# The order of the two halves of P beside the FFN: POOL's half first, VectorE's second

## The chip, the cores and the metric

The kernel runs on one core of a Trainium2 chip. The metric is the device time of one execution in microseconds; of the kernel before there are three: 980.2 (median), 979.35 and 982.82. One further execution was profiled; it took 981.36 us, and its span, from the first to the last instruction in the trace, is 979.6 us. In the profile PE is TensorE's matmuls and PEld its weight loads, DVE is VectorE, ACT is ScalarE, POOL is GpSimd and SP the engine that issues most DMAs. L468 is line 468 of the kernel's file.

## What is computed

Attention whose mask comes from a hash, and on its output an FFN with a gate:

```python
# q, k, v: (4, 8, 768, 64) f32; proj: (64, 6); w_in: (512, 2048); w_out: (2048, 512)
q_bits = einsum('bhsd,dk->bhsk', q, proj) > 0        # 6 bits: 64 buckets; k alike
mask   = q_bucket[:, :, :, None] == k_bucket[:, :, None, :]
scores = where(mask, (q @ k.T) / 8, -1e9)
attn   = exp(scores - max) ; attn /= attn.sum() + 1e-9
x      = (attn @ v) as (3072, 512)                    # tokens x (heads * 64)
h      = x @ w_in
out    = (h * clip(h + 3, 0, 6) / 6) @ w_out
```

All is float32. The kernel multiplies float32 numbers as pairs: a high part, which is the number rounded to the type that TensorE reads (`fp32r` in the profile), and a low part, the rest. A product is the sum of high and low terms, so before each product an engine makes the high part with a copy and another the low part with a subtraction.

## The kernel before

Attention is cut into blocks g of 128 queries of one head: 6 blocks a head, 32 heads, 192 blocks. P is the 128 x 768 tile of exponentials of one block. The FFN is cut into chunks of 256 tokens, each of 16 steps over d_ff, 128 columns a step (`gemm1` L642, the gate L664 and L665, its two parts L670 and L671, `gemm2` L680 to L685). The FFN of the first batch runs early; that of the later ones runs beside the attention of the blocks behind block 102 (`GT`), one FFN step to each attention step k, in the function `beside_ffn`. The order of all instructions on PE, DVE, ACT and POOL is that of the program, written out by hand; only DMAs are issued with dependences of their own. An engine takes its instructions in this order and waits at each until its operands are there.

In a step k of `beside_ffn` with k of at least 102 this is issued, in this order:

- if k is odd, `values_whole(u)`: the product of V with P of the two blocks 2u and 2u + 1 (2u + 3 is k or, at the ends, less). On PE it is 12 matmuls into one accumulator (L501): the high parts of P, keys 0 to 383 (half c = 0), then keys 384 to 767 (c = 1), then the low parts in the same order;
- `lowest(k + 2)` on VectorE (L385): scores from the accumulator to SBUF, with their minimum;
- the two parts of the gate of the FFN step before: copy on ACT (L670), subtraction on VectorE (L671);
- `exponential(k + 2)` on ACT (L397), and on VectorE the transpose of its result in blocks of 32 x 32 (`flip`, L418), whose result goes to DRAM and comes back with whole rows and columns exchanged (tiles `px` and `spare` by turns, `move`);
- `split_p(k - 1, c)` for c = 0 and then c = 1: from the tile that came back it makes the high part `ph` with a copy on ACT (L464), and the low part `pl` of half 0 on VectorE (L468) and of half 1 on POOL (L466). POOL's subtraction is issued at once, VectorE's is kept in the list `lows` and issued behind both copies (`split_lows`);
- `gemm1` of the FFN step on PE; the output of attention, if there is one (L528 to L531); in every sixth step the hash of the next head (`hash_qk` on PE, and after the gate `bits`, L341 on VectorE);
- `gemm2` of the FFN step before on PE, and the gate of this one: L664 on ACT and L665 on VectorE;
- `scores(k + 3)` on PE (L376, L378), DMAs, and every second or third step a subtraction for the next head's q and k on POOL (L318).

Each pair of blocks u has four tiles, `ph` and `pl` for each half; each of the names has two buffers, so that the tiles of a pair take over those of the pair before, once its products have read them.

Of the kernel before, what the change touches and what calls it, by code (L numbers as in the profile page):

```python
# [43 lines left out]
def lsh_attention_moe(  # L44
# [10 lines left out]
    nc = tc.nc  # L55
# [3 lines left out]
    KT = S // P  # L59
    HW = S // 2  # L60
    QT = HW // P
# [31 lines left out]
    def bank(shape, name: str, tag: str | None = None):  # L93

        nonlocal turn
        if tag is None:
            tag = ("pt", "pu")[turn % 2]
            turn += 1
        return ps.tile(shape, F32, name=name, tag=tag, bufs=2)
# [280 lines left out]
    def lowest(g: int):  # L380

        s = scs.pop(g)
        m = sp.tile([P, 1], F32, name=f"m{g}", tag="m", bufs=4)
        pr_ = sp.tile([P, 2, HW], F32, name=f"p{g}", tag="p", bufs=2)
        nc.vector.tensor_scalar(  # L385
            out=pr_[:], in0=s[:, :, :HW], scalar1=CAP, scalar2=None,
            op0=ALU.min, op1=ALU.min, accum_out=m[:],
        )
        probs[g] = pr_, m

    def exponential(g: int):
        i, t = divmod(g, KT)
        b, h = divmod(i, H)
        if b not in sms:
            sms[b] = sp.tile([P, KT, H], F32, name=f"sms{b}", tag="sms", bufs=2)
        pr_, m = probs[g]
        nc.scalar.activation(  # L397
            pr_[:], pr_[:], AF.Exp, bias=m[:], scale=-1.0, accum_out=sms[b][:, t, h : h + 1]
        )
# [4 lines left out]
    def transp(g: int, c: int):  # L404
        pt = pts[g, c] = bank([P, QT, P], f"pt{g}_{c}")
        for x in range(QT):
            nc.tensor.transpose(pt[:, x], probs[g][0][:, c, x * P : (x + 1) * P], ident[:])  # L407
        if c:
            del probs[g]
# [30 lines left out]
    def split_p(g: int, c: int, third: bool):  # L440

        nonlocal halves
        u, w = divmod(g, 2)
        if w == 0:
            extra = third and halves % 3 == 1
            halves += 1
            if extra and lent:
                both = [x[:, :S] for x in lent]
            else:
                both = [  # L450
                    sp.tile([P, NCC * TC if extra else S], F32R, name=f"{x}{u}_{c}", tag=f"x{x[1]}" if extra else x, bufs=1 if extra else 2)[:, :S]
                    for x in ("ph", "pl")
                ]
            parts[u, c] = [x.rearrange("p (x w q) -> p x w q", x=QT, w=2) for x in both]
        hi, lo = (x[:, :, w] for x in parts[u, c])
        engine = nc.vector
        if g < GT:
            pt = pts.pop((g, c))[:]
        else:
            pt = moved[g].rearrange("p (i x a) -> p x i a", i=4, x=KT)[:, c * QT : (c + 1) * QT]  # L460
            hi, lo = (x.rearrange("p x (i a) -> p x i a", i=4) for x in (hi, lo))
            if c:
                engine = nc.gpsimd
        nc.scalar.copy(hi, pt)  # L464
        if engine is nc.gpsimd:
            engine.tensor_sub(lo, pt, hi.bitcast(F32))  # L466
        else:
            lows.append(lambda: engine.tensor_sub(lo, pt, hi.bitcast(F32)))  # L468
# [3 lines left out]
    def split_lows():  # L472
        for f in lows:
            f()
        lows.clear()
# [18 lines left out]
    def values_whole(u: int):  # L494
        vv = vvs[2 * u // KT]
        acc = accs[u] = bank([P, 2 * P], f"acc{u}")
        both = [parts.pop((u, c)) for c in range(2)]
        for part in range(2):
            for kt in range(KT):
                c, x = divmod(kt, QT)  # L500
                nc.tensor.matmul(  # L501
                    acc[:], lhsT=vv[:, kt], rhs=both[c][part][:, x],
                    start=(part == 0 and kt == 0), stop=(part == 1 and kt == KT - 1),
                )

    adds = []

    def add():
        for _, to, of in adds:
            nc.gpsimd.dma_start(out=to, in_=of, accum_op=ALU.add)  # L510
        adds.clear()

    def output(un: int):
        nonlocal vdone
        i, u = divmod(un, KT // 2)
        b, h = divmod(i, H)
        o = (h % 2) * D
        acc = accs.pop(un)

        if u != 1:  # L520
            outs[i] = sp.tile([P, 4 * P if u == 0 else 2 * P], F32, name=f"y{i}_{u}", tag=f"y{u}", bufs=1)
        y = outs[i][:, 2 * P :] if u == 1 else outs[i][:, : 2 * P]

        r = slice(o, o + D)
        r2 = slice(D - o, 2 * D - o)
        last_head = h == H - 1 and (b > 0 or u == 2)
        if last_head:
            nc.scalar.copy(y[r], acc[r2])  # L528
            nc.vector.tensor_add(y[r], acc[r], y[r])
        else:  # L530
            nc.scalar.copy(y, acc[:])  # L531
        if u or last_head:
            c = slice(2 * u * P, 2 * (u + 1) * P) if last_head and b else slice(0, 4 * P) if u == 1 else slice(4 * P, S)
            to = xs[b][h * D : (h + 1) * D, c]

            with tc.issue_after(copied.ins):
                dma(out=to, in_=y[r] if last_head else outs[i][r])
            if not last_head:
                adds.append((i, to, outs[i][r2]))
        vdone = 2 * un + 2  # L540
# [38 lines left out]
    def multiply():  # L579
        for f in muls:  # L580
            f()
        muls.clear()
# [468 lines left out]
    def value_whole():  # L1051
        nonlocal vnext
        values_whole(vnext // 2)
        vnext += 2

    def value_half():
        nonlocal vnext
        u, c = divmod(vnext, 2)
        vnext += 1
        values(u, c)  # L1060
        return c == 1
# [14 lines left out]
    with tc.manual_schedule(engines={ET.PE, ET.DVE, ET.Activation, ET.Pool}):  # L1076
# [9 lines left out]
        def go(part: str):  # L1086
            if stage == part:
                next(fill, None)
# [3 lines left out]
        def beside_ffn(k: int):  # L1092

            nonlocal paced, stage, held
            held = False
            if k < GT:
                for c in range(2):
                    transp(k, c)  # L1100
                exponential(k + 1)
            for _ in range(2):
                u = vnext // 2
                if u < NS // 2 and (2 * u < GT or k % 2 and k >= 2 * u + 3):
                    if vnext % 2 == 0 and k >= GT:
                        value_whole()
                        through.append(u)
                        break
                    if value_half():
                        through.append(vnext // 2 - 1)  # L1110
                if k < GT:
                    break
            if k == GT:
                opening.pop()()
            if k + 2 < NS and k >= GT:
                lowest(k + 2)
            go("A")
            if k < GT:
                for c in range(2):
                    split_p(k, c, False)  # L1120
                split_lows()
                while through:
                    output(through.pop(0))
                flip(k + 1)
            if k + 2 < NS:
                if k < GT:
                    lowest(k + 2)
                exponential(k + 2)
            paced = True
            multiply()  # L1130
            if k + 2 < NS:
                flip(k + 2)
            if GT <= k - LT < NS:
                for c in range(2):
                    split_p(k - LT, c, False)
            split_lows()
            go("B")
            if k == NS + LT:
                homes.clear()
            while through and (through[0] < vnext // 2 - 1 or k % 2 == 0 or k < GT):  # L1140
                output(through.pop(0))
            hashed = k + LA < NS and (k + LA) % KT == 4 and (k + LA) // KT + 1 < NJ
            if hashed:
                hash_qk((k + LA) // KT + 1)
            go("C")
            if hashed:
                bits((k + LA) // KT + 1)
            if k + LA < NS:
                lead(k + LA)
            if moves:  # L1150
                moves.pop(0)()
            if GT <= k + 1 < NS:
                move(k + 1)

            place_in_chunk = (k - GT) % NFC
            if subs and (k % 2 and (k < GT or place_in_chunk != NFC - 1) or k > GT and place_in_chunk == 0):
                subs.pop(0)()
            go("D")
            if k % KT in (1, 3):
                add()  # L1160

        for k in range(NS + LT + 2):
# [3 lines left out]
            end = GB if k < GB else NS  # L1166
# [65 lines left out]
            if k + 1 == GB:  # L1232
                first = first_ffn(lambda part: ahead(GB, part))
# [57 lines left out]
```

## Time and profile before

| | |
|---|---|
| median of 3 executions | 980.2 us |
| the profiled execution | 981.36 us |
| its span | 979.6 us |
| stretch in which attention and FFN run side by side | 405 to 806 us |
| granted TensorE clock, mean of the span | 0.998 |
| L466 (POOL's low part) in the stretch: 86, mean of one | 1388 ns (from `spare`), 1378 ns (from `px`) |
| L468 (VectorE's low part) in the stretch: 86, mean of one | 519 ns, 517 ns |
| L464 (copies on ACT) in the stretch: 172, mean of one | 504 ns |

A row of the timeline has the start in us from the start of the span, the length in us, the engine, the line, the operation, what it writes and reads, the shapes, and how many alike are merged; the brackets hold the idle time of the engine ahead of it and what ended that. A row of the groups has busy us and mean ns behind the first bar, and idle us and its releasers behind the second. A row of the waits has who waited for whom, the total in us, how often, and the longest. The chain of waits is followed back from the last instruction, each step to what released it.

### The profile page before, as it was taken

Reading aid. Unit: us, or ns where it says so; the run is one execution under the profiler, and the core shown is the slowest. Engines: PE = TensorE matmul, PEld = TensorE weight load, DVE = VectorE, ACT = ScalarE, POOL = GpSimd, SP = SyncE. Lnnn points to the kernel's source line nnn. Section 1 sums busy time; section 2 is a strip of 40 time slices with the busy share of each in tenths; the row PEclk is TensorE's granted clock in tenths of the full one; section 3 lists DMA queues with packets and bytes.
Section 4 is the critical chain, followed back from the end, with each engine's and each line's share of the span. In section 5 each row is a group of like instructions: output and inputs, shape, how many; then the busy total and the mean of one; then the engine's idle time right before and its main releaser. Section 6 shows DMA issues by size and latency. Waiting matters only on the chain.

```text
span 979.6 us, 19386 instructions
## 1 busy us (share of the span) xinstructions
PE 953.1 (97%) x6306; PEld 874.4 (89%) x6306; DVE 715.7 (73%) x1462; ACT 626.7 (64%) x1421; POOL 479.2 (49%) x498
## 2 busy tenths in 40 slices
PE   8999999999999998899999999999999999999997
PEld 7999888999989998799889888998999899899896
DVE  7999988888569998777777777877777874343422
ACT  6898875656478897567766666766766664333332
POOL 6777744656537775355555545546556542000000
PEclk9999999999999999999999999999999999999999
DMA  4566579100035554687797787797797772101000
GB/s 118 138 165 174 132 229 376 46 2 1 6 121 130 117 114 118 184 246 235 217 274 231 230 244 234 225 272 231 233 267 228 220 222 78 43 1 44 1 22 22
DMA packets 113116, 151.65 MB, mean 155 GB/s; under 512 B 13764, under 2 KB 82116, under 8 KB 113016
## 3 DMA queue, kind: packets, MB, share of 16 engines
q1 hardware_dynamic: 108456, 144.79, 48.8%
q0 software_dynamic: 4560, 5.64, 4.6%
q8 instruction: 50, 0.82, 0.4%
q14 instruction: 50, 0.41, 0.1%
HBM read 77.34 MB, written 53.61 MB: 134 GB/s over the span
## 4 chain that ended last, share of the span: by engine, by line
PE 77%; DVE 9%; issue 4%; POOL 3%; DMA 3%; ACT 2%; SPq 1%; DVEq 0%; ACTq 0%; POOLq 0%
PE h L642 25%; PE po L685 6%; PE po L680 6%; PE po L681 6%; PE acc L489 6%; PE acc L501 5%; PE s L376 5%; PE pt L407 5%; PE s L378 5%; DVE p L385 3%; DVE pl L468 2%; POOL pl L466 2%; DVE qq L341 1%; DMA px<-fd 1%; SPq L78 1%
## 5 line engine op out<-in xcount | busy, mean ns | idle before, releaser
L397 ACT ACTIVATE p<-p,m 128x768 f32<-128x768 f32 x192 | 180.2, 938 | 97.0 <-DVE p L385 91.3
L385 DVE TENSOR_SCALAR_CACHE_REDUCE p<-s 128x768 f32<-128x768 f32 x192 | 183.0, 953 | 45.4 <-PE s L378 30.8
L665 DVE SCALAR_TENSOR_TENSOR h<-g,h 128x256 f32<-128x256 f32 x192 | 81.9, 427 | 95.2 <-ACT g L664 93.5
L664 ACT ACTIVATE g<-h,three 128x256 f32<-128x256 f32 x192 | 90.8, 473 | 91.4 <-PE h L642 89.7
L642 PE MATMUL h<-xh,w 128*128 128x256 f32 x1024 | 146.8, 283 | 1.6 <-ACT xh L631 1.6
L642 PEld LDWEIGHTS h<-xh,w 128*128 128x128 f32 x1024 | 135.5, 189 | 5.1 <-ACT xh L631 1.8
L418 DVE STREAM_TRANSPOSE p<-p 128x768 f32<-128x768 f32 x90 | 88.0, 978 | 60.3 <-ACT p L397 60.3
L466 POOL TENSOR_TENSOR pl<-spare,ph 128x384 fp32r<-128x384 f32 x45 | 62.1, 1381 | 119.0 <-ACT ph L464 82.8
L376 PE MATMUL s<-kk,qq 76*128 76x384 f32 x384 | 101.4, 345 | 4.8 <-DVE qq L341 3.0
L468 DVE TENSOR_TENSOR pl<-pt,ph 128x384 fp32r<-128x384 f32 x196 | 100.0, 550 | 3.6 <-ACT ph L464 3.0
L670 ACT CAST gb<-h 128x256 fp32r<-128x256 f32 x141 | 52.4, 372 | 76.1 <-DVE h L665 43.1
L378 PE MATMUL s<-kk,qq 128*128 128x384 f32 x384 | 100.6, 343 | 0.0
L681 PE MATMUL po<-w,gb 128*128 128x512 f32 x250 | 98.4, 394 | 0.0
L680 PE MATMUL po<-w,gb 128*128 128x512 f32 x250 | 98.4, 394 | 0.0
L466 POOL TENSOR_TENSOR pl<-px,ph 128x384 fp32r<-128x384 f32 x45 | 61.3, 1362 | 75.2 <-ACT ph L464 66.0
L464 ACT CAST ph<-pt 128x384 fp32r<-128x384 f32 x196 | 85.9, 472 | 15.1 <-PE pt L407 13.1
L216 POOL TENSOR_TENSOR w<-wr,w 128x128 fp32r<-128x128 f32 x128 | 71.8, 591 | 45.3 <-ACT w L210 42.4
L407 PE MATMUL pt<-ident,p 128*128 128x128 f32 x612 | 86.0, 274 | 3.6 <-DVE pl L468 2.7
L407 PEld LDWEIGHTS pt<-ident,p 128*128 128x128 f32 x612 | 71.7, 141 | 11.2 <-PE pt L407 2.5
L376 PEld LDWEIGHTS s<-kk,qq 76*128 76x128 f32 x384 | 65.7, 190 | 17.9 <-DVE qq L341 8.0
L642 PE MATMUL h<-xl,w 128*128 128x256 f32 x512 | 81.5, 281 | 0.0
L685 PE MATMUL po<-w,gb 128*128 128x512 f32 x250 | 78.7, 395 | 0.0
(153 smaller groups left out, 2130.9 us busy)
## 6 DMA issues: line engine op xcount, KB each, us to landing
fd<-p SPq DMA_DIRECT2D x90, 384.0 KB, 3.0
spare<-fd SPq DMA_DIRECT2D x180, 96.0 KB, 2.6
px<-fd SPq DMA_DIRECT2D x180, 96.0 KB, 3.2
kk<-qq SPq DMA_DIRECT2D x62, 192.0 KB, 3.3
wr<-in_w_in SPq DMA_DIRECT2D x16, 512.0 KB
wr<-in_w_out SPq DMA_DIRECT2D x16, 512.0 KB, 7.5
raw<-in_qkT SPq DMA_DIRECT2D x19, 384.0 KB, 3.8
vr<-in_v SPq DMA_DIRECT2D x32, 192.0 KB, 3.4
```

What stands on the lines that cost most here:

```text
L376: nc.tensor.matmul(s[:, c, :HW], lhsT=q1[:KM, us], rhs=half(k1[:KM], c), start=True, stop=False)
L378: nc.tensor.matmul(s[:, c, :HW], lhsT=q2[:, us], rhs=half(k2, c), start=False, stop=True)
L385: nc.vector.tensor_scalar(out=pr_[:], in0=s[:, :, :HW], scalar1=CAP, scalar2=None, op0=ALU.min, op1=ALU.min, accum_out=m[:],)
L397: nc.scalar.activation(pr_[:], pr_[:], AF.Exp, bias=m[:], scale=-1.0, accum_out=sms[b][:, t, h : h + 1])
L407: nc.tensor.transpose(pt[:, x], probs[g][0][:, c, x * P : (x + 1) * P], ident[:])
L466: engine.tensor_sub(lo, pt, hi.bitcast(F32))
L468: lows.append(lambda: engine.tensor_sub(lo, pt, hi.bitcast(F32)))
L642: nc.tensor.matmul(hp, lhsT=wi[:, wp, wc], rhs=x[cc][xp], start=(k == 0 and cc == 0), stop=(k == 2 and cc == NCC - 1),)
L664: nc.scalar.activation(r[:], hp, AF.Relu, bias=three[:], scale=1.0)
L680: nc.tensor.matmul(po[u], lhsT=gh[:, us], rhs=wo[:, 0], start=(fc == 0), stop=False)
L681: nc.tensor.matmul(po[u], lhsT=gh[:, us], rhs=wo[:, 1], start=False, stop=False)
L685: nc.tensor.matmul(po[u], lhsT=gl[:, us], rhs=wo[:, 0], start=False, stop=(fc == NFC - 1))
```

## The change

In every step of `beside_ffn` from block 102 on the halves are split in the order c = 1, c = 0, and `values_whole` multiplies in that order too, the high parts of half 1 and half 0 and then the low parts of half 1 and half 0. The `start` and `stop` flags of the accumulation move to the new first and last matmul. The rest of the program is as it was: the subtraction of half 0 is still issued behind both copies, and in the earlier part of the kernel the halves keep their order.

```diff
@@ values_whole
         both = [parts.pop((u, c)) for c in range(2)]
+        first, end = (0, 1, 0), (1, 0, QT - 1)
         for part in range(2):
-            for kt in range(KT):
-                c, x = divmod(kt, QT)
-                nc.tensor.matmul(
-                    acc[:], lhsT=vv[:, kt], rhs=both[c][part][:, x],
-                    start=(part == 0 and kt == 0), stop=(part == 1 and kt == KT - 1),
-                )
+            for c in (1, 0):
+                for x in range(QT):
+                    nc.tensor.matmul(
+                        acc[:], lhsT=vv[:, c * QT + x], rhs=both[c][part][:, x],
+                        start=(part, c, x) == first, stop=(part, c, x) == end,
+                    )
@@ beside_ffn
             if GT <= k - LT < NS:
-                for c in range(2):
+                for c in (1, 0):
                     split_p(k - LT, c, False)
             split_lows()
```

## The prediction

> **What bounds the kernel now.** I read the page first, for which engine is full, then the stretch from 405 to 806 us, the only one in which the changed lines run side by side with the FFN.
>
> ```profile
> PE 953.1 (97%) x6306; PEld 874.4 (89%) x6306; DVE 715.7 (73%) x1462; ACT 626.7 (64%) x1421; POOL 479.2 (49%) x498
> ```
> ```profile
> 405.00:806.00 401.00, 394.80 (x2534) 360.63 (x2532) 304.31 (x588) 266.27 (x619) 217.39 (x189) 1.00 0.81 238
> ```
>
> In that stretch (the second row, busy us of PE, PEld, DVE, ACT and POOL in turn) PE is busy 394.8 of 401 us, so TensorE bounds by its own work; VectorE is busy 304.3. But a share says nothing of order, so next the timeline of two neighbouring steps (start, length, engine, line, in brackets the idle time before and its releaser).
>
> ```profile
> 722.06 0.91 ACT L464 CAST ph<-px 128x384 fp32r<-128x384 f32 x2
> 722.19 0.98 DVE L418 STREAM_TRANSPOSE p<-p 128x768 f32<-128x768 f32 x1 [0.64 <-ACT p L397]
> 723.06 1.42 POOL L466 TENSOR_TENSOR pl<-px,ph 128x384 fp32r<-128x384 f32 x1 [2.29 <-ACT ph L464]
> 723.09 0.52 DVE L468 TENSOR_TENSOR pl<-px,ph 128x384 fp32r<-128x384 f32 x1
> 723.64 0.43 DVE L665 SCALAR_TENSOR_TENSOR h<-g,h 128x256 f32<-128x256 f32 x1
> 723.98 0.95 DVE L385 TENSOR_SCALAR_CACHE_REDUCE p<-s 128x768 f32<-128x768 f32 x1
> 726.04 0.98 DVE L418 STREAM_TRANSPOSE p<-p 128x768 f32<-128x768 f32 x1 [0.76 <-ACT p L397]
> 726.94 0.52 DVE L468 TENSOR_TENSOR pl<-spare,ph 128x384 fp32r<-128x384 f32 x1
> ...
> 728.69 0.96 DVE L385 TENSOR_SCALAR_CACHE_REDUCE p<-s 128x768 f32<-128x768 f32 x1 [0.90 <-PE s L378]
> ```
>
> Follow VectorE: minimum (L385), then the exponential on ACT that it must wait for, transpose (L418), low part (L468), gate (L665), next minimum. It is a ring (the transpose's releaser is the exponential, L397): from L468 at 723.09 to L468 at 726.94 are 3.85 us, with no idle time but the wait for the exponential, which sits inside the ring. The only slack of the pair is the 0.90 before L385 at 728.69, where TensorE's scores are late. So a second ring runs almost as slowly as TensorE, and L468, which the change delays, is a link of it.
>
> Every sixth step also hashes the next head, and there VectorE is not slack at all:
>
> ```profile
> 577.51 0.52 DVE L468 TENSOR_TENSOR pl<-spare,ph 128x384 fp32r<-128x384 f32 x1
> 577.95 0.42 DVE L665 SCALAR_TENSOR_TENSOR h<-g,h 128x256 f32<-128x256 f32 x1
> 578.40 1.08 DVE L341 TENSOR_SCALAR qq<-z,thr,val 44x768 fp32r<-44x768 f32 x1
> 579.54 0.62 PE L376 MATMUL s<-kk,qq 76*128 76x384 f32 x2 [0.33 <-DVE qq L341]
> 580.56 0.96 DVE L385 TENSOR_SCALAR_CACHE_REDUCE p<-s 128x768 f32<-128x768 f32 x1 [1.07 <-PE s L378]
> ```
>
> L468, L665 and L341 follow each other, TensorE's scores wait for L341, and VectorE's next 1.07 us of idle time wait for those scores. That idle time moves along with L468; it hides nothing.
>
> **The change, part by part.** No instruction is added or removed: per step two copies, one subtraction on POOL and one on VectorE, and in every second step 12 products. Only orders change: the two ACT copies, then the products.
>
> **The copies.** A copy's mean comes from its group (busy us, mean ns, idle before):
>
> ```profile
> L464 ACT CAST ph<-px 128x384 fp32r<-128x384 f32 x86 | 39.3, 504 | 1.4 <-DMA px<-fd 1.3
> ```
>
> In the step above the pair of copies starts at 722.06. One takes 0.50 us; POOL started 0.09 after the end of the pair (722.97 to 723.06). So POOL would start at 722.56 + 0.09 = 722.65 instead of 723.06, 0.41 sooner. VectorE's copy now ends second, at 722.97, but L468 waits for the transpose until 723.09 anyway, so that wait costs nothing. What costs is another thing, which the durations show.
>
> ```profile
> 573.15 0.56 DVE L468 TENSOR_TENSOR pl<-px,ph 128x384 fp32r<-128x384 f32 x1 [0.18 <-ACT ph L464]
> 573.66 1.02 POOL L466 TENSOR_TENSOR pl<-px,ph 128x384 fp32r<-128x384 f32 x1 [1.85 <-ACT ph L464]
> ```
> ```profile
> 142.01 0.73 POOL L632 TENSOR_TENSOR px<-xr,px 128x256 fp32r<-128x256 f32 x1 [5.05 <-ACT px L631]
> 142.27 0.76 DVE L632 TENSOR_TENSOR px<-xr,px 128x256 fp32r<-128x256 f32 x1 [0.16 <-ACT px L631]
> ...
> 146.66 0.74 POOL L632 TENSOR_TENSOR plx<-xr,phx 128x256 fp32r<-128x256 f32 x1 [3.92 <-ACT phx L631]
> 146.93 0.76 DVE L632 TENSOR_TENSOR plx<-xr,phx 128x256 fp32r<-128x256 f32 x1 [0.19 <-ACT phx L631]
> ```
>
> POOL's subtraction takes 1.02 us where VectorE's is nearly done when it starts (573.66), and 1.42 where both start together (723.06): in the second case POOL stood still while VectorE ran. Both subtract two tiles that lie in SBUF. At 142.01 and 146.66 it is the other way round: POOL starts 0.26 us ahead, keeps its own time (0.73), and VectorE takes 0.76 and ends 0.29 after POOL, twice. So whichever gets hold first makes the other stand. Today VectorE gets it, though POOL's record starts 0.03 earlier; with the change POOL starts 0.44 ahead of VectorE (722.65 against 723.09), more than the 0.26 that was enough. I take it that **POOL goes first and VectorE stands**.
>
> The Trainium skill, SBUF — State Buffer, section "SBUF: two separate sides", says that the port pair shared by VectorE and GpSimd is locked for a whole instruction by whichever starts first, which speaks against this change. The rows agree, except that a lead of 0.03 us in the records doesn't decide. [...]
>
> **The price per step.** VectorE's groups in the stretch (busy us, mean ns, then idle before them and its releasers):
>
> ```profile
> L418 DVE STREAM_TRANSPOSE p<-p 128x768 f32<-128x768 f32 x87 | 85.1, 978 | 58.4 <-ACT p L397 58.4
> L385 DVE TENSOR_SCALAR_CACHE_REDUCE p<-s 128x768 f32<-128x768 f32 x88 | 83.9, 953 | 30.3 <-PE s L378 28.9 <-DMA fd<-p 1.1
> L665 DVE SCALAR_TENSOR_TENSOR h<-g,h 128x256 f32<-128x256 f32 x87 | 37.1, 426 | 3.9 <-ACT g L664 2.4
> L671 DVE TENSOR_TENSOR gb<-h,gb 128x256 fp32r<-128x256 f32 x86 | 36.2, 421 | 1.0 <-ACT gb L670 0.6
> L468 DVE TENSOR_TENSOR pl<-spare,ph 128x384 fp32r<-128x384 f32 x43 | 22.3, 519 | 1.3 <-ACT ph L464 1.3
> L468 DVE TENSOR_TENSOR pl<-px,ph 128x384 fp32r<-128x384 f32 x43 | 22.2, 517 | 0.2 <-ACT ph L464 0.2
> L341 DVE TENSOR_SCALAR qq<-z,thr,val 44x768 fp32r<-44x768 f32 x14 | 15.2, 1086 | 0.5
> L632 DVE TENSOR_TENSOR xl<-xr,xh 128x256 fp32r<-128x256 f32 x20 | 8.9, 504 | 1.3 <-ACT xh L631 1.2
> ```
>
> POOL: 722.65 + 1.02 = 723.67. VectorE ends 0.29 later for 256 columns; it has 384 here, and 128 more columns cost 0.10 (L671 to L468, 421 to 517 ns) to 0.145 (L468 to L385, 517 to 953 over 384 columns), I take 0.12. End at 723.67 + 0.41 = 724.08, before it was 723.61: **0.47 us later** (0.45 to 0.50 by those ends). Where the copies come late, the transpose is long over, and L468 ended 573.71; it would end at 572.61 + 0.50 + 0.09 + 1.02 + 0.41 = 574.63, 0.92 later, 0.45 more than usual. Such steps are 6 in the stretch:
>
> ```profile
> ACT ph L464 <- DMA spare<-fd: 2.6, 3, 1.1
> ...
> ACT ph L464 <- DMA px<-fd: 1.3, 3, 0.6
> ```
>
> **What hides it.** In the table's last columns the 58.4 before the transpose are the ring's own. The other rows give 30.3 + 3.9 + 1.0 + 1.3 + 0.2 + 0.5 + 1.3 = 38.5 us. The gap of 580.56 stands in ten of the fourteen hashing steps, the first and the last of them:
>
> ```profile
> 413.67 0.96 DVE L385 TENSOR_SCALAR_CACHE_REDUCE p<-s 128x768 f32<-128x768 f32 x1 [1.07 <-PE s L378]
> ...
> 720.12 0.96 DVE L385 TENSOR_SCALAR_CACHE_REDUCE p<-s 128x768 f32<-128x768 f32 x1 [1.08 <-PE s L378]
> ```
>
> That is 10 x 1.07 = 10.7 of rigid idle time (in the other four VectorE has FFN work there). Free: 27.8.
>
> **The products.** Today they wait for POOL's part, in the chain of waits and in PE's weight loads:
>
> ```profile
> 723.60 1.55 PE acc L501 x12
> ...
> 759.89 1.43 PE acc L501 x12
> ```
> ```profile
> PEld acc L501 <- POOL pl L466: 4.0, 10, 0.5
> ```
>
> 12 products take 1.43 without a wait, 0.12 each, as in some ten of the 43 steps with products; ten waits are long, 4.0 in all; in the other 23 or so they take about 1.55. After the change POOL's part is asked for behind 6 products instead of 9, 3 x 0.12 = 0.36 sooner, and is there 0.81 sooner (723.67 against 724.48). So the waits go, some 23 x 0.12 + 4.0 = 6.8 us, but I count that as nothing: TensorE then stands at the scores for a VectorE that is later still. If that cover were gone, it would be the faster rival below. The last three products now need VectorE's part, there at 724.08, and are due at 723.60 + 9 x 0.12 = 724.68: no wait of its own. The buffers of the halves are freed in the order in which they are filled again, so no new wait comes from them.
>
> **The sum.** 86 x 0.47 = 40.4, and 6 x 0.45 = 2.7, less 27.8 of idle time: +15.3. The profiled execution took 981.36 (span 979.6 and 1.8 around it), 1.2 over the median of 980.2; so 996.7 for such an execution and **995.5** as the median. With 0.45 per step the sum is +13.6 (993.8), with 0.50 it is +17.9 (998.1), and where the 8.2 us of idle time outside L385 don't serve it is 15.3 + 8.2 = +23.5 (1003.7): 993 to 1004.
>
> **Rivals.**
> - VectorE still gets hold first, so POOL starts earlier and stands as now. For: today it wins from 0.03 behind. Against: the rows at 142 and 146. POOL's end moves 0.41, TensorE asks 0.36 sooner, 43 x 0.05 = 2.2 gained: 978.0. Then the change does hardly anything.
> - Not slower but faster: VectorE isn't made to stand here (POOL is quick and VectorE too), and the waits of the products fall away whole: 980.2 - 6.8 = 973.4. It needs both 142 rows to be something else. It decides below a delay of about 0.3 us a step, which is 27.8 / 86.
> - The rigid gaps serve after all, because hashing can shift: 43.1 - 38.5 = +4.6, 984.8. Against: the wait of L376 for L341.
> - POOL's next subtraction takes hold ahead of the standing VectorE. It would stand 1.84 us more in 26 steps (rows below), 48 on top of the forecast, 1043. For: POOL's queue follows at once in these steps. Against: at 142.27 and 146.93 VectorE went on as soon as POOL ended; but nothing was queued on POOL there.
>
> ```profile
> L318 POOL TENSOR_TENSOR kk<-raw,qq 64x768 fp32r<-64x768 f32 x13 | 24.0, 1843 | 1.1
> L318 POOL TENSOR_TENSOR qq<-raw,qq 64x768 fp32r<-64x768 f32 x13 | 23.9, 1840 | 1.0
> ```
>
> **How the numbers follow.** The forecast 0.67, the first rival 0.10, the faster one 0.12, the gaps that serve after all 0.08, the queue on POOL 0.03. Predicted: 995.5. The range leaves out the faster case and the costliest one, 0.15: 977.5 to 1004; the forecast's own is 993 to 1004. A measurement of this kernel can tell about 0.5% (4.9 us) from no change: faster 0.12, same 0.10 + 0.08 = 0.18, slower 0.67 + 0.03 = 0.70.
>
> **What would show it.** Right: L466 at about 1.02 us instead of 1.38, starting 0.4 before L468; L468 at 0.9 to 1.0 instead of 0.52; VectorE's busy time in the stretch up by some 40 us and its idle time before L385 down to the hashing steps; no wait of L501 for POOL; more waits of the scores for L341. Wrong: L468 still at 0.52 (first rival if L466 keeps 1.4, the faster one if it falls to 1.02), or L468 long and the stretch hardly longer, which would mean that idle time I called rigid gave way.

## The result and the profile after

The changed kernel takes 993.36 us (median of 4, 992.64 to 996.24), the kernel before 980.01 (median of 4): a ratio of 1.0133, 95% interval 1.0113 to 1.0153, so 13.3 us slower. The profiled execution took 992.64 us, its span is 990.9, 11.3 more than before. The spans differ by less than the medians because this execution is the lowest of its four, while the profiled one of before (981.36) lies above its median. Behind `values_whole` all lines have moved by one: L501 is now L502, the gate's L664 and L665 are L665 and L666.

The stretch in which attention and FFN run side by side now ends at about 817 us. In the view by windows (busy us of PE, PEld, DVE, ACT, POOL):

```profile
405.00:817.00 412.00, 392.90 (x2528) 359.63 (x2527) 338.61 (x587) 265.64 (x618) 196.27 (x189) 1.00 0.78 232
```

TensorE has the same work in 11 us more. VectorE's busy time has gone from 304.3 to 338.6 and POOL's from 217.4 to 196.3, though neither has an instruction more or less (1462 and 498 in the whole program, as before). The groups of the stretch say whose time that is (busy us and mean ns, then idle us before and its releasers):

```profile
L468 DVE TENSOR_TENSOR pl<-px,ph 128x384 fp32r<-128x384 f32 x43 | 44.4, 1032 | 0.4 <-ACT ph L464 0.4
L468 DVE TENSOR_TENSOR pl<-spare,ph 128x384 fp32r<-128x384 f32 x43 | 42.8, 995 | 0.1
L385 DVE TENSOR_SCALAR_CACHE_REDUCE p<-s 128x768 f32<-128x768 f32 x87 | 82.4, 947 | 12.9 <-PE s L378 10.7 <-DMA spare<-fd 1.2 <-DMA fd<-p 0.7
L418 DVE STREAM_TRANSPOSE p<-p 128x768 f32<-128x768 f32 x87 | 85.1, 979 | 58.5 <-ACT p L397 58.5
```
```profile
L466 POOL TENSOR_TENSOR pl<-px,ph 128x384 fp32r<-128x384 f32 x43 | 44.2, 1027 | 73.1 <-ACT ph L464 49.6 <-DMA spare<-fd 10.5 <-DMA kk<-qq 5.7
L466 POOL TENSOR_TENSOR pl<-spare,ph 128x384 fp32r<-128x384 f32 x43 | 43.7, 1015 | 135.9 <-ACT ph L464 110.0 <-DMA px<-fd 12.5 <-DMA xs<-y 7.1
```

The two subtractions have changed places: L466 takes 1.02 us instead of 1.38, L468 1.01 instead of 0.52. VectorE's idle time before L385, 30.3 before, is down to 12.9; that before the transpose, the wait for the exponential, is what it was. Two neighbouring steps on the timeline:

```profile
733.42 0.91 ACT L464 CAST ph<-px 128x384 fp32r<-128x384 f32 x2
733.55 0.98 DVE L418 STREAM_TRANSPOSE p<-p 128x768 f32<-128x768 f32 x1 [0.64 <-ACT p L397]
734.01 1.01 POOL L466 TENSOR_TENSOR pl<-px,ph 128x384 fp32r<-128x384 f32 x1 [2.84 <-DMA spare<-fd]
734.45 0.99 DVE L468 TENSOR_TENSOR pl<-px,ph 128x384 fp32r<-128x384 f32 x1
735.36 0.42 DVE L666 SCALAR_TENSOR_TENSOR h<-g,h 128x256 f32<-128x256 f32 x1
735.69 0.94 DVE L385 TENSOR_SCALAR_CACHE_REDUCE p<-s 128x768 f32<-128x768 f32 x1
...
738.64 0.98 DVE L468 TENSOR_TENSOR pl<-spare,ph 128x384 fp32r<-128x384 f32 x1
...
739.92 0.96 DVE L385 TENSOR_SCALAR_CACHE_REDUCE p<-s 128x768 f32<-128x768 f32 x1
```

POOL starts 0.59 behind the start of the copies, 0.44 ahead of VectorE, and keeps its own 1.01. VectorE's L468 ends at 735.44, 0.42 behind POOL's end at 735.02. The ring from L468 to L468 is 4.19 us (734.45 to 738.64) instead of 3.85, and the 0.90 of slack before the second L385 is gone: there is no bracket at 739.92. The waits of TensorE in the stretch:

```profile
PE s L376 <- DVE qq L341: 13.5, 14, 1.7
PE po L686 <- DVE gb L672: 3.0, 3, 1.2
```
```profile
PEld acc L502 <- POOL pl L466: 1.9, 6, 0.3
```

The scores of the hashing steps, the steps that hash the next head, waited 3.0 us in all for VectorE's L341 before:

```profile
PE s L376 <- DVE qq L341: 3.0, 5, 1.3
```

Now it is 13.5. The products wait for POOL 1.9 instead of 4.0, and the chain of waits shows most of them at about 1.43 us, a few at 1.47 to 1.59.

```profile
723.97 1.47 PE acc L502 x12
734.95 1.43 PE acc L502 x12
```

### The profile page after: what moved, and what is told of

It reads as the page before. It is cut to its first block, busy times and chain, and to the rows that moved or that the text cites. A ratio compares the mean times of both kernels' runs of the same rounds, so it can differ in the third digit from the quotient of the medians.

```text
span 990.9 us, 19382 instructions
## 1 busy us (share of the span) xinstructions
PE 952.5 (96%) x6306; PEld 873.7 (88%) x6306; DVE 753.6 (76%) x1462; ACT 626.8 (63%) x1421; POOL 458.0 (46%) x498
## 4 chain that ended last, share of the span: by engine, by line
PE 71%; DVE 11%; DMA 5%; POOL 4%; issue 4%; SPq 3%; ACT 2%; DVEq 0%; ACTq 0%; POOLq 0%
PE h L643 23%; PE acc L489 6%; PE po L681 5%; PE po L686 5%; PE po L682 5%; PE pt L407 5%; PE s L376 5%; PE acc L502 5%; PE s L378 4%; DVE pl L468 3%; DVE p L385 3%; SPq L78 3%; DVE qq L341 2%; POOL pl L466 2%; DMA px<-fd 2%
## 5 line engine op out<-in xcount | busy, mean ns | idle before, releaser
L385 DVE TENSOR_SCALAR_CACHE_REDUCE p<-s 128x768 f32<-128x768 f32 x192 | 182.4, 950 | 28.3 <-PE s L378 12.6
L666 DVE SCALAR_TENSOR_TENSOR h<-g,h 128x256 f32<-128x256 f32 x192 | 80.9, 422 | 90.6 <-ACT g L665 90.4
L665 ACT ACTIVATE g<-h,three 128x256 f32<-128x256 f32 x192 | 90.8, 473 | 89.6 <-PE h L643 89.0
L418 DVE STREAM_TRANSPOSE p<-p 128x768 f32<-128x768 f32 x90 | 88.1, 978 | 60.4 <-ACT p L397 60.4
L376 PE MATMUL s<-kk,qq 76*128 76x384 f32 x384 | 101.2, 344 | 15.3 <-DVE qq L341 13.5
L466 POOL TENSOR_TENSOR pl<-spare,ph 128x384 fp32r<-128x384 f32 x45 | 45.7, 1016 | 141.7 <-ACT ph L464 115.8
L468 DVE TENSOR_TENSOR pl<-pt,ph 128x384 fp32r<-128x384 f32 x196 | 100.0, 550 | 3.6 <-ACT ph L464 3.0
L464 ACT CAST ph<-pt 128x384 fp32r<-128x384 f32 x196 | 86.2, 473 | 14.8 <-PE pt L407 13.0
L686 PE MATMUL po<-w,gb 128*128 128x512 f32 x250 | 79.1, 397 | 3.0 <-DVE gb L672 3.0
L466 POOL TENSOR_TENSOR pl<-px,ph 128x384 fp32r<-128x384 f32 x45 | 46.2, 1027 | 75.8 <-ACT ph L464 52.3
```

The source lines that it names most:

```text
L376: nc.tensor.matmul(s[:, c, :HW], lhsT=q1[:KM, us], rhs=half(k1[:KM], c), start=True, stop=False)
L385: nc.vector.tensor_scalar(out=pr_[:], in0=s[:, :, :HW], scalar1=CAP, scalar2=None, op0=ALU.min, op1=ALU.min, accum_out=m[:],)
L665: nc.scalar.activation(r[:], hp, AF.Relu, bias=three[:], scale=1.0)
L686: nc.tensor.matmul(po[u], lhsT=gl[:, us], rhs=wo[:, 0], start=False, stop=(fc == NFC - 1))
```

## The experiments

Ratios are to the kernel before on the same chip, with the 95% interval; line numbers are those of each kernel's own file. "The copies" are the order of `split_p` in `beside_ffn`, "the products" that of `values_whole`.

### The two halves of the change, each alone

**e1_copies**: the copies exchanged, the products as before.

```diff
-                for c in range(2):
+                for c in (1, 0):
                     split_p(k - LT, c, False)
```

> The copies alone are exchanged (POOL's half first); the products keep the order of before. Theory 1 (POOL gets hold first and VectorE's subtraction stands, which lengthens VectorE's ring): the whole loss is here. L466 at 1.02 us, L468 at 1.0, no wait of the products for POOL in either order, time 990 to 995. Theory 2 (the loss comes from the products, which ask for POOL's part three matmuls sooner): POOL's part is earlier and asked for as before, so 973 to 980.

**e2_products**: the products exchanged (the whole change to `values_whole`), the copies as before.

```diff
-                for c in (1, 0):
+                for c in range(2):
                     split_p(k - LT, c, False)
```

> The products alone are exchanged; the copies keep the order of before. L466 at 1.38 and L468 at 0.52 as before by both theories. Theory 1 (VectorE stands): the loss of the change isn't here; POOL's part is asked for 0.36 us sooner with no earlier start, so about 33 of 43 products wait 0.36 longer, up to +12: 985 to 992, with waits of L502 for POOL in the trace and no lengthened L468. Theory 2 (the products' order costs): the same 985 to 992, so this run alone doesn't tell them apart; with e1 it does: by theory 2 e1 is at or under 980.

Measured: e1 995.47 us, 1.0153 (1.0133 to 1.0173), half a us above the range given; e2 989.43 us, 1.0092 (1.0076 to 1.0107). Both alone are slower, for different reasons. VectorE's group in e1, and TensorE's weight loads in e1 and e2:

```profile
L468 DVE TENSOR_TENSOR pl<-px,ph 128x384 fp32r<-128x384 f32 x43 | 44.1, 1025 | 0.5 <-ACT ph L464 0.5
```
```profile
PEld acc L501 <- DVE pl L468: 3.4, 10, 0.4
```
```profile
PEld acc L502 <- POOL pl L466: 16.1, 33, 0.7
```

With the copies alone the lengthened L468 and the whole loss are there; theory 2 falls. The products, in the order of before, now wait a little for VectorE's half, which they ask for first. With the products alone L468 is at 0.52, and 33 of the products wait for POOL's half, which they ask for three matmuls sooner and which comes no sooner. In the whole change that second cost is absent, since POOL is early: the losses don't add up, the change has that of the copies.

### POOL's subtraction in two pieces

**e3_pool_two**: as the changed kernel, with

```diff
         if engine is nc.gpsimd:
-            engine.tensor_sub(lo, pt, hi.bitcast(F32))
+            for r in (slice(0, 2), slice(2, 4)):
+                engine.tensor_sub(lo[:, :, r], pt[:, :, r], hi[:, :, r].bitcast(F32))
```

> As the changed kernel, but POOL's subtraction is two instructions of 192 columns. Theory 1 (hold for a whole instruction): VectorE gets in between them. The first piece is over some 0.6 us after its start, about when VectorE is ready, so L468 falls from 1.0 to 0.55 to 0.6, the second piece on POOL stands instead (0.6 to 1.0 us), POOL's part is there some 0.3 us earlier than in the kernel before, and the time falls back to 977 to 985. Rival (the two engines share bandwidth evenly, nobody stands): L468 stays near 1.0 and the time at 993.

Measured: 980.91 us, 1.0006 (0.9995 to 1.0016): the loss is gone. On its timeline:

```profile
723.17 1.48 POOL L467 TENSOR_TENSOR pl<-px,ph 128x192 fp32r<-128x192 f32 x2 [2.35 <-ACT ph L464]
723.61 0.57 DVE L469 TENSOR_TENSOR pl<-px,ph 128x384 fp32r<-128x384 f32 x1
```

VectorE starts 0.44 behind POOL, as in the changed kernel, on as many columns, but ends after 0.57 us, because POOL's first piece ends; the second piece stands instead, so that both pieces take 1.48. Nothing but the length of POOL's instruction differs between this kernel and the changed one. That settles that VectorE stands until POOL's instruction is over, and that this is the loss.

**e7_two_copies** and **e8_third_copies**: the products in the order of before, the copies exchanged, POOL's subtraction in pieces of 192 and 192 columns (the edit of e3), and of 128 and 256:

```diff
+            for r in (slice(0, 1), slice(1, 3)):
+                engine.tensor_sub(lo[:, r], pt[:, r], hi[:, r].bitcast(F32))
```

> The copies exchanged, the products in the order of before, and POOL's subtraction in two pieces of 192 columns. Theory 1 (hold for a whole instruction, the ring, and products that wait for POOL): VectorE stands for the first piece at most, L468 at 0.55 to 0.62; POOL's part is there 0.3 to 0.4 sooner than before and asked for as late as before, so the short waits of L502's products go: 972 to 978, a little faster than before. Rival (the number of VectorE's lengthened subtractions doesn't matter, any earlier start on POOL costs): 990 or more as in e1.

> As e7, with pieces of 128 and 256 columns. By theory 1 the first piece ends some 0.1 us before VectorE is ready, and VectorE gets in ahead of the second, so L468 is 0.52 to 0.55 and POOL's part some 0.1 later than in e7: 973 to 979, within 2 us of e7. If instead the second piece gets hold ahead of VectorE, L468 is 0.9 to 1.0 and the time 985 to 992.

Measured: e7 977.00 us, 0.9963 (0.9951 to 0.9974); e8 977.03 us, 0.9970 (0.9959 to 0.9980). Both are faster than the kernel before by about a third of a per cent. e7 differs from e3 in the order of the products alone, worth some 4 us by their ratios: half 1 is asked for last again, and TensorE's weight loads, which waited for it in e3 (first row), hardly do in e7 (second row).

```profile
PEld acc L503 <- POOL pl L467: 5.7, 11, 0.8
```
```profile
PEld acc L502 <- POOL pl L467: 0.2, 1, 0.2
```

In e8 VectorE doesn't stand any more:

```profile
723.44 1.57 POOL L467 TENSOR_TENSOR pl<-spare,ph 128x128 fp32r<-128x128 f32 x2 [2.27 <-PE h L643]
723.89 0.52 DVE L469 TENSOR_TENSOR pl<-spare,ph 128x384 fp32r<-128x384 f32 x1
```

### VectorE's half behind the gate

If VectorE only had something else to do while POOL subtracts, both could be quick. **e4_gate_between** issues the copy of half 0 and L468 behind the gate:

```diff
+            if GT <= k - LT < NS:
+                split_p(k - LT, 1, False)
...
             go("C")
+            if GT <= k - LT < NS:
+                split_p(k - LT, 0, False)
+                split_lows()
```

> As the changed kernel, but the copy and the subtraction of VectorE's half stand behind the gate of the FFN (L665 on ACT, L666 on VectorE) instead of ahead of it. VectorE's work is the same; while POOL subtracts, VectorE does the gate, which reads one operand from PSUM. Theory 1: L466 at 1.02 and L468 at 0.52 both, VectorE's ring as short as before, no wait of the products for POOL: 968 to 976, faster than both kernels. If the loss comes from the ACT queue or from the products' order instead, this changes nothing: 990 to 995.

Measured: 989.42 us, 1.0096 (1.0076 to 1.0116): a miss. L466 is at 1.02, as expected, and L468 at 0.64, where 0.52 was expected: in most steps POOL isn't quite done when it starts (724.01, with POOL running until 724.20). That doesn't explain the time. From transpose to transpose many pairs of steps come out 0.1 to 0.2 us shorter than in the kernel before, but at five beginnings of a chunk a step is 0.6 to 1.9 us longer, 7.4 in all. At one of them the timeline has

```profile
480.99 1.08 ACT L700 ACTIVATE ob<-po 128x512 f32<-128x512 f32 x2
481.63 1.82 POOL L318 TENSOR_TENSOR kk<-raw,qq 64x768 fp32r<-64x768 f32 x1
481.95 0.52 ACT L464 CAST ph<-px 128x384 fp32r<-128x384 f32 x1
482.50 1.36 DVE L468 TENSOR_TENSOR pl<-px,ph 128x384 fp32r<-128x384 f32 x1 [0.94 <-DMA kk<-qq]
482.52 0.62 PE L502 MATMUL acc<-ph,vv 128*128 128x256 f32 x3 [1.11 <-ACT ph L464]
```

The moved copy queues behind the storing of the finished chunk, and VectorE then stands behind another of POOL's subtractions, L318 (until 483.45; L468 ends at 483.86). **e6_gate_store** puts the half directly behind the gate, ahead of the storing:

```diff
                 split_g = gate(n, fc, hp, copy, nc.vector)
+                if behind_gate:
+                    behind_gate.pop()()
```

> As e4, but VectorE's half stands directly behind the gate, ahead of the copies that store a finished chunk (L700 of e4's file). Theory A on e4's miss (in the first step of a chunk the copy of half 0 queues behind 1.08 us of storing, VectorE then meets POOL's next subtraction and stands again): the jumps of 1.9 and 1.1 us at five chunk boundaries go, some 8 us, and the time is 979 to 983. Theory B (e4's loss is spread over all steps, because L468 behind the gate lengthens the ring by 0.13): 987 to 991.

Measured: 981.75 us, 1.0021 (1.0007 to 1.0035). Theory A on the miss holds: the five steps are at most 0.13 us longer than in the kernel before. What is left, 0.2% over that kernel, wasn't looked into further; the only step still more than half a us longer (1.29) is one in which a small addition of VectorE stands 1.81 us, as in the last section.

### The subtraction in the wait for the exponential

**e9_even_early**: orders as before, but in even steps both copies and subtractions are issued ahead of the exponential.

```diff
+            early = GT <= k - LT < NS and (k % 2 == 0)
+            if early:
+                for c in range(2):
+                    split_p(k - LT, c, False)
             go("A")
+            if early:
+                split_lows()
```

> The kernel before, orders of halves and products unchanged, but in even steps both copies and both subtractions are issued ahead of the exponential: VectorE's subtraction falls into its wait for the exponential, and POOL's part is there some 2 us sooner. Theory 1 (VectorE's ring and POOL's late part are what limits): the ring is up to 0.4 shorter in every second step and the products wait for nothing: 966 to 974. It falls if the transfers of P from DRAM come too late for the earlier copies (ACT then waits at L464 for px and the exponential with it): 980 to 995, with waits of L464 for DMA in the trace.

Measured: 995.09 us, 1.0159 (1.0132 to 1.0186). It fell for the reason that was named; the groups of ACT in its stretch and the waits of TensorE have

```profile
L464 ACT CAST ph<-px 128x384 fp32r<-128x384 f32 x86 | 39.8, 510 | 66.0 <-DMA px<-fd 66.0
```
```profile
PE po L680 <- ACT gb L670: 15.3, 15, 2.5
```

ACT waits 66 us at the copies, because P isn't back from DRAM, and TensorE 15.3 us for ACT's later copy L670. In the even steps L468 is lengthened too, to 0.87 us. So the run says nothing on what the ring would gain.

### The hashing steps

**e11_not_hashing** (changed kernel, but with the copies as before in the 14 hashing steps of the stretch) and **e12_hashing_only** (kernel before, but with the copies exchanged in these steps alone):

```diff
-                for c in (1, 0):
+                for c in (range(2) if k + LA < NS and (k + LA) % KT == 4 and (k + LA) // KT + 1 < NJ else (1, 0)):
                     split_p(k - LT, c, False)
```

> As the changed kernel, but in the steps that hash the next head (14 of 86 in the stretch) the copies are in the order of before. The delay of a step as measured in the changed kernel is 0.39 us. Theory 1 with rigid hashing steps (there VectorE's delay goes whole into the end, elsewhere idle time hides part of it): 14 x 0.39 = 5.4 us come back, 987 to 989. Rival (the loss is spread evenly over the 86 steps, 13.3 / 86 = 0.155 each): 2.2 come back, 991 to 992.

> As the kernel before, but in the steps that hash the next head the copies are exchanged; the products keep their order. Theory 1 with rigid hashing steps: 14 x 0.39 = 5.4 us more than before, 984 to 987. Rival (spread evenly): 2.2 more, 981.5 to 983. If hashing steps had slack like the others, 979.5 to 981.

Measured: e11 990.12 us, 1.0094 (1.0076 to 1.0112), e12 984.22 us, 1.0038 (1.0024 to 1.0052). So 1.0133 less 1.0094, some 3.8 us, come back in e11, with an uncertainty of 2.6, and 3.7 (2.4 to 5.1) are lost in e12: 0.27 a step, between both theories (990.12 lies between their ranges, 984.22 at the foot of theory 1's). In e12 TensorE's wait for L341 shows it, 3.0 before:

```profile
PE s L376 <- DVE qq L341: 6.6, 10, 1.8
```

A hashing step costs more than the mean of all steps (13.3 / 86 = 0.155), as e12's interval just says and e11's doesn't, and less than the full 0.39. That is a mean of two kinds. By the starts of L418 in the timelines of before and after, the ten steps with the gap of 1.07 us are each 0.34 to 0.51 us longer in the changed kernel, 0.44 in the mean, so they have no slack; of the other four, in which VectorE has FFN work, two are 0.22 and 0.24 longer and two 0.33 shorter. Why two are shorter isn't shown. All fourteen together are 4.2 us longer, in line with e11 and e12.

## Why the prediction was right

It gave 995.5 us, with 993 to 1004 for its own case; 993.36 was measured, at the lower edge. The mechanism was in the main the forecast one; that the number came within 2.1 us is in part luck, as the sum shows. By its steps:

- **POOL goes first and VectorE stands.** Right. POOL leads by 0.44 us as worked out (734.01 and 734.45), L466 and L468 exchange their lengths, and e3 shows the cause: with POOL's instruction cut in two, all else the same, the loss is gone. The first rival (VectorE still gets hold first) and the faster one (nobody stands) fall with L468 at 1.01. So does POOL's queue as a rival, by steps in which POOL's L318 follows at once:

```profile
719.10 1.01 POOL L466 TENSOR_TENSOR pl<-spare,ph 128x384 fp32r<-128x384 f32 x1 [1.09 <-ACT ph L464]
719.50 1.03 DVE L468 TENSOR_TENSOR pl<-spare,ph 128x384 fp32r<-128x384 f32 x1
720.20 2.04 POOL L318 TENSOR_TENSOR qq<-raw,qq 64x768 fp32r<-64x768 f32 x1
```

  L468 ends at 720.53, 0.42 behind POOL's L466 as elsewhere, and it is L318 that gets longer.
- **0.47 us a step.** Mis-sized. L468 is 0.50 longer, but from its start to that of the gate there are 0.91 (734.45 to 735.36) instead of 0.55 (723.09 to 723.64), 0.36 more. Behind an instruction that stood, the gate starts 0.08 before its end; before the change it started 0.03 after. With this step's 0.11 taken for all 86, 0.50 less 0.11 is 0.39, 33.5 us in all instead of 40.4; the mean over the steps in which the gate follows L468 directly, 0.94 instead of 0.54 from start to start, bears it out.
- **2.7 us for steps with late copies.** They hardly exist any more: ACT's idle time before L464 is 0.5 us in all, where it was 4.2.
- **27.8 us of idle time to hide it.** Nearly right. The idle time of VectorE outside the wait for the exponential was 38.5 and is 12.9 + 0.5 and 1.3 in the groups that aren't shown, 14.7; 23.8 were used. What TensorE leaves before L385, 10.7 us, is the 10.7 that were called rigid, and the ten steps with these gaps bear the whole delay, 0.44 a step. The other four hashing steps are what brings the mean of e12 down to 0.27.
- **The waits of the products count as nothing.** Right in the sum: most of them went, though 1.9 us are left where none were forecast, and TensorE lost more at L341 (13.5 instead of 3.0) and at L686 (3.0).
- **The sum.** With the measured terms 33.5 - 23.8 = +9.7, where the spans differ by 11.3. Of the forecast's +15.3 the delay was 9.6 too large (43.1 against 33.5) and the idle time 4.0; the two errors partly cancel.
- **Three steps without a term.** Once in each chunk of 16 steps VectorE makes a small addition on the row sums (L549, now L550) behind the gate. Before, it started ahead of POOL's L318 and stood only until L466 was over; in three of five places it now starts behind L318 and stands for it. First the rows before, then after:

```profile
447.52 1.43 POOL L466 TENSOR_TENSOR pl<-spare,ph 128x384 fp32r<-128x384 f32 x1 [2.41 <-ACT ph L464]
448.33 0.66 DVE L549 TENSOR_SCALAR rc<-sms 128x16 f32<-128x16 f32 x1
449.03 1.85 POOL L318 TENSOR_TENSOR kk<-raw,qq 64x768 fp32r<-64x768 f32 x1
```
```profile
449.75 1.84 POOL L318 TENSOR_TENSOR kk<-raw,qq 64x768 fp32r<-64x768 f32 x1 [0.56 <-ACT qq L304]
449.86 1.76 DVE L550 TENSOR_SCALAR rc<-sms 128x16 f32<-128x16 f32 x1
```

  The others are at 602.17 (1.48 us) and 681.50 (1.76). From transpose to transpose these three steps are 1.38, 1.33 and 1.38 us longer than before, 4.1 in all, while the first and the last transpose of the stretch are 11.55 us further apart. So over a third of the loss lies here: not L468's standing alone, but what its delay sets off behind it. In e3 the same addition takes 0.24 us (448.38), so cutting POOL's subtraction took this away too. All five additions of the stretch take 1.4 us more than before (5.3 against 3.9), since two got shorter; that may be most of the 1.6 that the sum is short of, but the balance isn't closed.

The lock for a whole instruction, which the prediction cited from the Trainium skill, SBUF — State Buffer, section "SBUF: two separate sides", agrees with e3: cutting POOL's instruction, not moving it, is what released VectorE (0.57 us instead of 0.99 in the rows shown).

## What to carry to other kernels

Before two engines are given the same moment for subtractions of two SBUF tiles, look in the trace at which of them stands today, and whether the one that will stand after the edit is a link of a ring. VectorE was 76% busy and bound nonetheless, because its ring of minimum, exponential, transpose, subtraction and gate had less idle time outside it than the edit asked for. Look also at what stands next in the queue of the engine that goes first: whatever the late engine does there may now have to stand for it too. Where a late engine has to come first, cut its instruction so that the other gets in between; that was worth 12.5 us here (993.36 to 980.91), and with the products' old order it beat the kernel before by 0.3%.

## What the runs showed of the hardware

- Which of the two goes first isn't decided by the recorded starts alone. With POOL's start 0.03 us ahead VectorE goes first (723.06 and 723.09 before the change); with 0.11 (449.75 and 449.86) and with 0.44 (734.01 and 734.45) POOL does.
- The standing passes on. With VectorE's L468 late, POOL's next instruction stands in its turn: the copy at L356 takes 0.83 us instead of 0.50, and half of L318's subtractions 2.04 instead of 1.84. First L356 before, then both groups in the changed kernel:

```profile
L356 POOL CAST vv<-vr 128x384 fp32r<-128x384 f32 x15 | 7.5, 501 | 0.0
```
```profile
L318 POOL TENSOR_TENSOR qq<-raw,qq 64x768 fp32r<-64x768 f32 x13 | 26.5, 2042 | 1.0
L356 POOL CAST vv<-vr 128x384 fp32r<-128x384 f32 x15 | 12.5, 834 | 0.0
```

- A tiny VectorE instruction with one SBUF tile as its input stands too: in e4 the addition to a 128 x 16 tile takes 1.80 us beside POOL's L318, in the changed kernel up to 1.76; where no subtraction of POOL runs beside it, it takes 0.17 (526.44 in the changed kernel).

```profile
598.41 2.03 POOL L318 TENSOR_TENSOR qq<-raw,qq 64x768 fp32r<-64x768 f32 x1
598.67 1.80 DVE L550 TENSOR_SCALAR rc<-sms 128x16 f32<-128x16 f32 x1
```

- The transpose at L418 doesn't: it keeps its 0.98 us, and POOL its 1.01, with the two running side by side for half of that time (733.55 and 734.01).
